# A planned attention kernel on one core: the accumulator stays open for zero-weight products until its last late tile, and the order of the work is planned anew

## The chip, the cores and the metric

The kernel runs on one core of one Trainium2 chip. The metric is the time of one execution on the device in microseconds (us); the median of the runs is what counts. A core has five engines with a queue of their own each, written here as the profile writes them: PE (TensorE, the matmuls; PEld are its weight loads), DVE (VectorE), ACT (ScalarE), POOL (GpSimd) and SP (SyncE, which here only issues DMAs).

## The reference

The input x is 2048 tokens of 512 values. Two mixers read it and a gate blends them:

```python
q, k, v = heads_of(x @ A_wqkv)                  # 32 heads of 16
p = softmax(q @ k.T * 16 ** -0.5)               # 2048 x 2048 for each head
a = merge(p @ v) @ A_wo
pq, pk = q_b @ w_phi, k_b @ w_phi               # q_b, k_b, v_b = heads_of(x @ B_wqkv)
phi = lambda y: concat(softmax(y), softmax(-y))
b = merge(phi(pq) @ (phi(pk).T @ v_b) / (phi(pq) @ phi(pk).sum())) @ B_wo
g = sigmoid((x * gate_w).sum(-1))
out = g * a + (1 - g) * b
```

Branch A is full attention: 32 x 2048 x 2048 exponentials. Branch B is linear attention with a small feature map.

## The kernel before

**Tiles.** The exponentials of branch A are cut into 2048 tiles of 128 keys by 512 queries (one head, one block of keys, one block of queries). Four heads stand side by side in TensorE's 32-row strips; a pack is four such tiles, one a head, and 16 packs with the same queries and heads (a group) share one accumulator, a bank of PSUM. There are 32 groups. For a tile the scores are one matmul of 512 columns (`_scores`, line 1044) into a PSUM bank, then comes the exponential, then the product with V (`_values`, line 1164) into the group's accumulator.

**Two ways to the exponential.** Most tiles go to ACT, in turn three and two tiles an instruction (`_exp`, line 1095), out of a ring of five PSUM banks: the next scores for a bank wait until ACT has read it. 248 tiles go to DVE instead, in batches of up to five (`_vector_batch`): DVE takes each tile's scores out of a bank (line 923), POOL cuts out a fraction (`_frac`, line 952), and DVE works out a cubic (lines 968, 969, 970) and adds it to the bits (line 938). Their products with V come in late: each is a TensorE instruction of its own, called `pvx`, that may stand in TensorE's order after the pack's own product `pv`. `SHARES` says how many tiles of each group DVE takes, `_plan_vector` spreads them over the group's packs. For group 8 it says 16, more than the 14 places there, so that two tiles of that group stand in the list twice: DVE works out 250 tiles for 248 that are used.

**The end of a group.** When the products of a group are in, its late ones too, DVE transposes the accumulator out of PSUM (line 1217), divides and transposes back (lines 1221 to 1229), and the bank is free. Three banks beside the ring serve accumulators, DVE's tiles, the projections, branch B and the output products in turn.

**The order.** No queue is written by hand. Every piece of work is an `Op` with a cost, a priority and what it depends on; `Plan.order` lists all of them engine by engine, each time taking of the operations that can start first the one with the lowest priority number, and the engines then run that order with semaphores between them. Priorities and earliest places are due times in packs, shifted by tables: `HURRY` and `EASE` (one entry for each of DVE's batches), `QEASE` (projections of queries), `LEASE` (branch B's parts), `OEASE` (output tiles), `OREL` (the last outputs), `ENDS` (the spread of DVE's tiles in the last group) and `REST` (the place of the batch of odd size).

**Zero-weight products.** Ahead of a TensorE operation `Plan.order` puts pads while the array's share of the last 2.7 us, by the plan's costs, is under 0.65 and the pad delays nothing due. A pad is four matmuls by a weight of zeros (`_fill`, line 1173), one a strip; it adds nothing to the sum. It goes into the accumulator that is open (`plan.open`), or, when none is, into a PSUM bank that is free by then; when there is neither, no pad is put. `_pv` opens the accumulator at the group's first `pv` and closes it at its last `pv`, though `pvx` of the group may still follow.

The plan's lines that decide on a pad:

```python
if have >= self.SHARE * self.SPAN or room > self.OVER * (o.kind == "col"):
    break
...
job, deps = self.open, []
if job is None:
    clear = [b for b in self.free_banks if b[1] <= first]
    if not clear:
        break
```

Of the kernel before, what the change touches and what calls it, by code (L numbers as in the profile page):

```python
# [70 lines left out]
class Plan:  # L71
# [12 lines left out]
    PORT = {"v_frac", "v_line", "v_sq", "v_cube", "v_out", "gate_z", "gate_h", "gate_b", "n_den", "n_mul", "kvbd", "b_grid", "b_rest",  # L84
            "b_max", "b_top", "b_octave", "b_square", "b_slope", "b_even", "b_odd", "b_part", "b_out", "b_sum", "b_ratio", "b_mul"}
    GUARD, GIVE, TAKE = 0.25, 0.1, 0.12
    MOVE = {}

    def __init__(self):
        self.ops = []  # L90
        self.now = -1
        self.free_banks = []
        self.loaded, self.turned = 0.0, False
        self.keep = None
        self.open = None
        self.pad = None
        self.live = False

    def op(self, eng, fn, cost, reads=(), writes=(), deps=(), name="", prio=0.0, rel=-99, kind="full",
           acquire=None, release=None, lat=None, array=None, groups=None):  # L100
        if name in self.MOVE:
            eng, cost = "POOL", self.MOVE[name](cost)
        o = Op(eng, fn, cost, name, prio, rel, kind, self.LAT[eng] if lat is None else lat, groups)
        found = {}
        for b in reads:
            for w in b.writers:
                found[id(w)] = w
        for b in writes:
            for w in b.readers or b.writers:
                found[id(w)] = w  # L110
            if b.readers:
                for w in b.writers:
                    found[id(w)] = w
        for d in deps:
            if d is not None:
                found[id(d)] = d
        found.pop(id(o), None)
        o.deps = list(found.values())
        for b in reads:
            b.readers.append(o)  # L120
        for b in writes:
            b.writers, b.readers = [o], []
        o.acquire, o.release = acquire, release
        o.array = cost if array is None else array
        self.ops.append(o)
        return o
# [265 lines left out]
class _Kernel:  # L392
# [13 lines left out]
    VREL0 = 5  # L406
    FIRST = (2, 2)
    LAST = (4,)
    OREL = 0
    ENDS = 11  # L410
    POOL = 0.00084
    SOONER = "_cube"
    TAIL = 2
    REST = 48
    HURRY = (0, 9.6, 3.1, -5.4, 16.2, -6.1, 0, -3.2, 10.5, 1.0, -8.4, 1.5, -3.1, 0.6, 12.0, 0, 9.6, 12.6, 0, -8.4, 6.7, 11.7,
              7.3, 0.7, -7.6, 2.9, 0.1, 0, 3.9, 0.3, 13.7, 4.0, 0, 3.9, -14.1, -5.6, -2.1, 7.4, 4.3, -1.8, -2.7, 18.1, -9.4,
              5.8, 4.8, 3.9, -6.0, 0, 0, 0, 0, 0, 0, 0, 0, 0, 0, 0, 0, 0)
    QEASE = (0, 4.2, -1.3, -2.9, 5.7, 0.3, 9.3, 7.6, 5.5, 9.6, -1.4, -2.2, -1.6, 9.1, 3.3, 2.1)
    LEASE = (-2.3, 3.2, 8.7, -2.0, 0, -20.0, -1.6, -2.5, -9.6, -3.3)
    OEASE = (-0.2, -4.3, 8.5, -1.3, 2.6, -5.0, 14.2, -2.3, 10.6, -2.1, 6.7, 3.8, 0.9, 0, 0, 0)  # L420
    EASE = (0, -0.9, 0, 6.0, -3.1, 3.7, 3.4, 3.9, 4.6, -1.9, -1.0, 0.1, 12, 8.0, 5.5, -12.1, -3.2, 8.6, 12, 9.8, 0, -1.0, -9.5,
              -3.3, -14, 0, 9.6, -2.8, -0.4, -10.7, 0, 10.0, -8.8, 5.2, -5.7, -4.3, -10.6, 0, -0.6, -3.0, 9.6, 3.5, -3.4, 12,
              12, -14, -4.8, 0, -0.2, 4.8, 0, -4.5, -1.6, 0, 0, 4.2, 0, 0, 0, 0)
    NBANK = 8

    def __init__(self, nc, A_x, A_wqkv, A_wo, B_wqkv, B_w_phi, B_wo, gate_w, out):
        self.nc = nc
        self.x2d = A_x.flatten_outer_dims()
        self.A_wqkv, self.A_wo = A_wqkv, A_wo
        self.B_wqkv, self.B_w_phi, self.B_wo = B_wqkv, B_w_phi, B_wo  # L430
        self.gate_w, self.out2d = gate_w, out.flatten_outer_dims()
        self.S = self.x2d.shape[0]
        self.NT = self.S // TOK
        self.NQC = self.S // QCH
        self.NPACK = self.NQC * 8 * self.NT
        self.plan = Plan()

    def build(self):
        with ExitStack() as ctx:
            self._memory(ctx)  # L440
            p = self.plan
            p.pad = lambda ot: lambda e: self._fill(e, ot)
            p.free_banks = [(b, 0.0, []) for b in range(self.NRING, self.NBANK)]
            self._loads()
            self._consts()
            self._projections()
            self._branch_b()
            self._attention()
            for o in p.order()["PE"]:
                for i in o.strips[1]:  # L450
                    o.strips[0].final[i] = o
            p.finals = self.stores
            p.emit(self.nc, ctx)
# [336 lines left out]
    def _proj_q(self, qc, cp, bank=None):  # L790
        n = qc * 4 + cp
        due = 32 * n - self.QDUE + self.QEASE[n]
        s0 = 2 * (n % (self.NQS // 2))
# [66 lines left out]
                name="gate_b", prio=24))  # L860
        self.b_hB.writers = parts

    SHARES = (0, 2, 4, 6, 2, 0, 5, 5, 16, 0, 9, 13, 4, 13, 11, 3, 11, 13, 6, 9, 9, 6, 12, 4, 11, 11, 8, 5, 12, 12, 14, 10)

    def _share(self, g):

        return self.SHARES[g]

    def _plan_vector(self):
# [9 lines left out]
        for k in range(n):  # L879
            at = (2 * k + 1) * self.ENDS // (2 * n)  # L880
            self.away.append(4 * (self.NT * last + 4 * (at // 3) + at % 3 + 1) + 3)
        left = len(self.away) - sum(self.FIRST) - sum(self.LAST)
        sizes = [self.NB] * (left // self.NB)
        sizes[self.REST:self.REST] = [left % self.NB] * (left % self.NB > 0)
        sizes = [*self.FIRST, *sizes, *self.LAST]
# [16 lines left out]
    def _vector_batch(self, number, units, due, step):  # L902
# [26 lines left out]
        n = NB * QCH  # L929
        prio = units[0] / 4 - self.VPRIO + self.HURRY[number]  # L930
        for name, cost, fn, reads, writes in self._cubic(flat(vt), flat(vf), flat(vu), n, b_vt, b_vf, b_vu):
# [170 lines left out]
    def _pv(self, p):  # L1102
        NT = self.NT
        g = p // NT
        a, kt, n = self._acc(p)
        for hook in self.hooks.get(p, ()):
            hook()
        qc, g8 = divmod(g, 8)
        block = self._block(p)
        deps, src = list(self.b_V[g8 // 2][p % NT // 4 if block is None else kt].writers), {}  # L1110
        values = list(deps)
        for u in range(4 * p, 4 * p + 4):
            if u in self.place:
                deps.append(self.exps[self.in_group[self.place[u]]])
                src[u % 4] = self.ET[:, self.place[u] % self.NSLOT, :]
        if kt == 0:
            self.ot[a] = Job()
            self.ot[a].part = block is not None
            deps += [x for u, xs in self.bits.items() if self._acc(u // 4)[0] == a - 1 for x in xs]
        else:  # L1120
            deps.append(self.pvs[p - 1])
        ot = self.ot[a]

        def run(e):
            for _ in range(o.filled):
                self._fill(e, ot)
            return self._values(e, ot, p, src, o)
        o = self.plan.op("PE", run, self._wide(4 * p), reads=[self.b_zero], deps=deps, name=f"pv{p}", prio=p + 2.5, kind="col",
                         acquire=None if kt else ot, array=0.0533 * len(src), groups=tuple(src))
        def commit(_):  # L1130
            if kt == 0:
                plan.open, plan.keep, plan.live = ot, None, True
            elif kt >= self.KEEP - NT + n and a + 1 in self.ot and all(x.start is not None for x in mine):
                plan.keep = self.ot[a + 1]
            if kt == n - 1:
                plan.open = None
        plan = self.plan
        mine = [x for u, xs in self.bits.items() if self._acc(u // 4)[0] == a for x in xs]
        o.on_commit = commit
        o.strips = (ot, tuple(src))  # L1140
        o.urgent = p >= self.NPACK - 3
        o.filler = 2 if kt and p < self.NPACK - 1 else 0
        self.pvs.append(o)
        for u in range(4 * p, 4 * p + 4):
            if u not in self.place:
                tile, made, buf = self.theirs[u]
                x = self.plan.op("PE", None, self._wide(u) - 0.13,
                                 deps=[o] + values, reads=[buf], name="pvx", prio=p + 2.6,
                                 kind="col", array=0.0533, groups=(u % 4,))
                x.fn = lambda e, u=u, tile=tile, x=x: self._values(e, ot, p, {u % 4: tile}, x)  # L1150
                x.strips = (ot, (u % 4,))
                self.late.append(x)
        if kt == n - 1:
            self._norm_a(g, [o] + self.late, ot, block and block[0] if block else None)
            self.late = []

# [417 lines left out]
    def _out_last(self, qc):  # L1574
# [3 lines left out]
        for tt in range(4):  # L1578
            t = 4 * qc + tt
            job, first = self.outs[t]  # L1580
            rel = self.NPACK - NT + 4 * tt + self.OREL
            due = self.NPACK - NT + 4 * tt + 6
# [71 lines left out]
```

## Time and profile before

| | us |
|---|---|
| median of 3 runs | 831.44 |
| the three runs | 830.63, 831.44, 832.70 |
| the profiled execution | 832.89 |
| its span, first to last instruction | 831.0 |
| ACT busy | 817.2 |
| PE busy, as modelled | 799.8 |
| DVE busy | 785.8 |
| POOL busy | 127.0 |
| mean granted clock of PE | 0.991 |

One execution was profiled, and it is slower than each of the three runs. Its span leaves out 1.89 us that lie around the instructions. The span is cut into 40 slices on the page, with a digit of busy tenths for each engine and one for the clock that PE was granted. Groups of instructions are listed by source line with their busy time, the mean of one, and the idle time of the engine just before them with what ended it. ACT is the busiest engine, and all but 2.3 us of its busy time are the 720 exponentials of line 1095. A PE that is busy in the profile need not be at its peak, since the ends of matmuls are modelled.

### The profile page before, as it was taken

The page shows a single profiled execution, that of the slowest core. Times are in us where ns is not written, and L with a number is a line of the kernel's source. Part 1 is how long each engine was busy: PE and PEld are TensorE (multiplying, and loading weights), DVE is VectorE, ACT ScalarE, POOL GpSimd, SP SyncE. Part 2 cuts the span into 40 slices and gives each one's busy share as a digit, 9 for nine tenths or more (in the row PEclk, how much of TensorE's full clock was granted, in tenths as well). Part 3 has the DMA queues.
Part 4 walks back from the last instruction along what each step waited for, and adds up shares of the span by engine and source line. Part 5 has one row for each costly group of instructions (what it writes and reads, how often), then busy time and mean ns, then how long its engine had stood idle before and what let it go on. Part 6 is the DMA issues. An engine that isn't in the chain of part 4 may idle for free.

```text
span 831.0 us, 19239 instructions
## 1 busy us (share of the span) xinstructions
PE 799.8 (96%) x8526; PEld 263.4 (32%) x8526; DVE 785.8 (95%) x1041; ACT 817.2 (98%) x725; POOL 127.0 (15%) x111
## 2 busy tenths in 40 slices
PE   9999999999989999999999999999999999999898
PEld 4323333333222222233222322223322223322244
DVE  6999999999998999999999999999999999999997
ACT  7999999999989999999999999999999999999997
POOL 3001100010112221112211212202122211122210
PEclk9999999999979999999999999999999999999999
DMA  9500000000000000031000310003110003110000
GB/s 244 165 6 8 1 8 2 1 8 1 6 2 2 8 1 3 8 65 21 1 2 10 79 23 8 8 2 65 26 21 8 2 2 64 27 27 1 2 2 28
DMA packets 49027, 19.99 MB, mean 24 GB/s; under 512 B 38704, under 2 KB 48944, under 8 KB 48944
## 3 DMA queue, kind: packets, MB, share of 16 engines
q1 hardware_dynamic: 48272, 18.58, 9.8%
q8 instruction: 66, 1.08, 0.5%
q10 hardware_dynamic: 672, 0.20, 0.1%
q14 instruction: 17, 0.14, 0.1%
HBM read 6.31 MB, written 2.10 MB: 10 GB/s over the span
## 4 chain that ended last, share of the span: by engine, by line
ACT 72%; DVE 20%; PE 6%; POOL 1%; issue 0%; DVEq 0%
ACT ET L1095 72%; DVE vu L938 3%; DVE vt L923 2%; PE ps L1044 2%; DVE vu L970 1%; DVE vf L969 1%; PE ps L1164 1%; DVE bq L1328 1%; POOL vf L952 1%; DVE VB L1312 1%; PE ps L1173 1%; DVE vt L1382 1%; DVE vu L968 1%; DVE bq L1420 1%; PE ps L720 1%; DVE V L822 1%
## 5 line engine op out<-in xcount | busy, mean ns | idle before, releaser
L1095 ACT ACTIVATE ET<-ps 128x1536 bf16<-128x1536 f32 x720 | 814.9, 1371 | 4.4 <-PE ps L1044 3.8
L1044 PE MATMUL ps<-qT,kT 32*128 32x512 bf16 (+2 forms) x2250 | 322.5, 367 | 25.0 <-ACT ET L1095 17.3
L1173 PE MATMUL ps<-kT,zero 128*32 128x512 bf16 (+1 forms) x2824 | 236.5, 386 | 0.0
L952 POOL TENSOR_SCALAR vf<-vt 128x1536 f16<-128x1536 uint8 (+1 forms) x96 | 118.9, 1254 | 651.4 <-DVE vu L938 365.4
L1164 PE MATMUL ps<-ET,V 128*32 128x512 bf16 (+2 forms) x1970 | 196.8, 368 | 1.0 <-DVE T L1217 0.5
L1044 PEld LDWEIGHTS ps<-qT,kT 32*128 32x128 bf16 x2250 | 85.8, 91 | 305.6 <-ACT ET L1095 203.0
L923 DVE TENSOR_SCALAR vt<-ps 128x512 uint32<-128x512 f32 x246 | 159.7, 680 | 14.8 <-PE ps L1044 12.3
L938 DVE SCALAR_TENSOR_TENSOR vu<-vt,vu 128x2560 int16<-128x2560 uint32 (+3 forms) x51 | 138.8, 2721 | 0.6
L1173 PEld LDWEIGHTS ps<-kT,zero 128*32 128x32 bf16 x2824 | 62.5, 95 | 98.9 <-issue 77.4
L1164 PE MATMUL ps<-vu,V 128*32 128x512 bf16 (+1 forms) x278 | 92.4, 364 | 0.1
L969 DVE TENSOR_TENSOR vf<-vf 128x2560 f16<-128x2560 f16 (+3 forms) x53 | 74.5, 1405 | 0.5
L970 DVE TENSOR_TENSOR vu<-vu,vf 128x2560 f16<-128x2560 f16 (+3 forms) x53 | 74.4, 1404 | 0.5
L1164 PEld LDWEIGHTS ps<-ET,V 128*32 128x32 bf16 x1970 | 54.7, 96 | 60.1 <-issue 32.4
L720 PE MATMUL ps<-WB,xT 128*128 128x512 bf16 x192 | 56.6, 383 | 0.6
L968 DVE TENSOR_SCALAR vu<-vf 128x2560 f16<-128x2560 f16 (+3 forms) x53 | 41.3, 780 | 3.1 <-POOL vf L952 2.9
L720 PE MATMUL ps<-xT,WA 128*128 128x512 bf16 (+1 forms) x124 | 35.1, 379 | 0.0
L1164 PEld LDWEIGHTS ps<-vu,V 128*32 128x32 bf16 x278 | 24.7, 96 | 19.3 <-issue 14.5
L1217 DVE STREAM_TRANSPOSE T<-ps 128x512 f32<-128x512 f32 (+1 forms) x35 | 23.2, 664 | 4.0 <-PE ps L1164 3.8
L1328 DVE TENSOR_SCALAR bq<-ps 128x512 bf16<-128x512 f32 x32 | 21.1, 677 | 2.0 <-PE ps L720 2.0
L720 PEld LDWEIGHTS ps<-WB,xT 128*128 128x128 bf16 x192 | 14.2, 97 | 26.9 <-issue 15.1
L816 PE MATMUL ps<-WA,xT 128*128 128x128 bf16 x256 | 18.8, 220 | 0.2
L1382 DVE TENSOR_TENSOR vt<-vt,brec 128x4096 bf16<-128x4096 bf16 (+1 forms) x10 | 18.6, 1857 | 0.0
(106 smaller groups left out, 426.6 us busy)
## 6 DMA issues: line engine op xcount, KB each, us to landing
qT<-qraw SPq DMA_DIRECT2D x120, 16.0 KB, 1.8
xn<-in_A_x_dram SPq DMA_DIRECT2D x3, 512.0 KB, 6.0
WB<-in_B_wqkv_dram SPq DMA_DIRECT2D x3, 512.0 KB, 4.9
out_dram<-WB SPq DMA_DIRECT2D x12, 128.0 KB, 1.8
WA<-in_A_wqkv_dram SPq DMA_DIRECT2D x3, 384.0 KB, 4.5
xn<-in_A_x_dram SPq DMA_DIRECT2D x2, 256.0 KB, 3.7
WoA<-in_A_wo_dram SPq DMA_DIRECT2D x1, 512.0 KB, 5.7
WoB<-in_B_wo_dram SPq DMA_DIRECT2D x1, 512.0 KB, 6.5
```

What stands on the lines that cost most here:

```text
L720: mm = op("PE", lambda e, c=c: e.matmul(self._bank(job)[:, 0:n], lhs(c), rhs(c), start=(c == 0), stop=(c == 3)), self.c_pe(n), reads=reads ...
L923: parts.append(op("DVE", lambda e, j=j, job=job: e.tensor_scalar(vt[:, j, :], self._bank(job), SCALE * LOG2E * 2.0 ** 24, 2.0 ** 31, op0=A ...
L938: self.last_out = o = op("DVE", lambda e: e.scalar_tensor_tensor(out=flat(vu).bitcast(I16), in0=flat(vt), scalar=2.0 ** -17, in1=flat(vu), ...
L952: "POOL", lambda e, a=at, n=n: e.tensor_scalar(vf[:, a:a + n, :], vt[:, a:a + n, :].bitcast(U8).rearrange("p n (q h) -> p n q h", h=4)[:, ...
L968: lambda e: e.tensor_scalar(vu, vf, CUBE, SQUARE, op0=ALU.mult, op1=ALU.add), [b_vf], [b_vu]),
L969: ("_sq", two, lambda e: e.tensor_tensor(vf, vf, vf, ALU.mult), [b_vf], [b_vf]),
L970: ("_cube", two, lambda e: e.tensor_tensor(vu, vu, vf, ALU.mult), [b_vf, b_vu], [b_vu]),
L1044: ins = e.matmul(out[u][:, cols], self.kT[32 * i:32 * i + 32, cp, kt * TOK:(kt + 1) * TOK], self.qT[32 * i:32 * i + 32, s, q], start=True, ...
L1095: o = plan.op("ACT", lambda e: e.activation(self.ET[:, a % NS:a % NS + n, :], self.ps[:, a % NR:a % NR + n, :], ACT.Exp, scale=SCALE), sel ...
L1164: ins = e.matmul(self._bank(ot)[32 * i:32 * i + 32, to], self.V[:, kt, g8 // 2, v0:v0 + 32], tile[:, cols], start=first and j == 0, stop=o ...
L1173: ins = e.matmul(self._bank(ot)[32 * i:32 * i + 32, lo:QCH], self.zero[:], self.kT[:, 0, lo:QCH], start=False, stop=False, tile_position=( ...
L1328: [lambda e, b, k=k: e.tensor_scalar(bq[:, k].rearrange("p (g s v) -> p g s v", g=8, s=2)[:, :, 0, :], b.rearrange("p (g v) -> p g v", g=8 ...
```

## The change

Three things change: `_pv` closes a group's accumulator only when the last of its late products has been placed; `Plan` can shift the priority of single operations by name and number (`NUDGE`, 65 entries); and all the tables of the order hold other numbers. Two knobs without use (`MOVE`, `NBANK`) go. `SHARES` now sums to 244 instead of 246, with no group over 14.

```diff
-        if name in self.MOVE:
-            eng, cost = "POOL", self.MOVE[name](cost)
+        n = self.made[name] = self.made.get(name, 0) + 1
+        prio += self.nudge.get((name, n), 0.0)
...
-    OREL = 0
-    ENDS = 11
+    OREL = 3
+    ENDS = 10
...
-    REST = 48
-    HURRY = (0, 9.6, 3.1, -5.4, 16.2, -6.1, 0, -3.2, 10.5, 1.0, -8.4, 1.5, -3.1, 0.6, 12.0, 0, 9.6, 12.6, 0, -8.4, 6.7, 11.7,
...
+    REST = 53
+    HURRY = (0.5, -7.6, 5.1, -6.5, 6.3, -11.8, 0, -8.0, 0, -17.8, -0.4, -1.2, -12.9, 25, 0, 8.1, 12.3, 0, 0.4, 10.0, 3.8, -1.8,
...
+    NUDGE = {
+        'b_max': {11: 3.7, 23: 22.2, 67: 10.7, 74: -19.5, 79: 13.2},
...
+        'pq': {34: 13.8, 40: 29.9, 43: -1.4, 53: -11.9, 69: -25.9, 73: 8.8, 77: 14.1, 85: -7.9, 88: -0.9, 101: 13.5,
+            120: 13.9},
...
+        'vqk': {75: 4.6, 78: -22.3, 124: 17.0, 130: -21.7, 149: 19.2, 156: 14.5},
+    }
...
-    SHARES = (0, 2, 4, 6, 2, 0, 5, 5, 16, 0, 9, 13, 4, 13, 11, 3, 11, 13, 6, 9, 9, 6, 12, 4, 11, 11, 8, 5, 12, 12, 14, 10)
+    SHARES = (0, 2, 4, 6, 0, 5, 2, 8, 10, 5, 11, 10, 8, 8, 9, 12, 9, 10, 2, 9, 6, 11, 9, 14, 7, 10, 5, 13, 11, 7, 12, 9)
...
-            if kt == n - 1:
+            if kt == n - 1 and not late:
                 plan.open = None
-        plan = self.plan
+        plan, late = self.plan, []
...
         if kt == n - 1:
+            late = list(self.late)
+
+            def close(_):
+                if plan.open is ot and all(x.start is not None for x in late):
+                    plan.open = None
+            for x in late:
+                x.on_commit = close
```

The computation, the tiles and the formulas are the same.

More of the change, by code (lines that the diff above doesn't have):

```diff
@@ L86 @@
     GUARD, GIVE, TAKE = 0.25, 0.1, 0.12
-    MOVE = {}
     def __init__(self):
@@ L91, in __init__ @@
         self.now = -1
+        self.made, self.nudge = {}, {}
         self.free_banks = []
@@ L413 @@
     TAIL = 2
-    REST = 48
-    HURRY = (0, 9.6, 3.1, -5.4, 16.2, -6.1, 0, -3.2, 10.5, 1.0, -8.4, 1.5, -3.1, 0.6, 12.0, 0, 9.6, 12.6, 0, -8.4, 6.7, 11.7,
[L416 to L424, printed above, removed]
+    REST = 53
+    HURRY = (0.5, -7.6, 5.1, -6.5, 6.3, -11.8, 0, -8.0, 0, -17.8, -0.4, -1.2, -12.9, 25, 0, 8.1, 12.3, 0, 0.4, 10.0, 3.8, -1.8,
+              -7.4, 0.7, 7.3, 25, 8.8, 25, 5.8, -6.9, 7.6, 3.4, -25, -14.5, 1.2, -7.3, -7.5, -20.6, -17.2, 21.6, -12.2, -4.6,
+              0, 10.0, -0.9, -12.6, 11.2, -4.7, -4.7, 0.8, 0, 0, 0, 0, 0, 0, 0, 0, 0, 0)
@@ new lines @@
+    QEASE = (0, -10, -4.8, 6.8, 6.6, 10.5, 16, 11.0, -7.8, 7.8, -3.9, -6.4, -9.2, 10.5, 8.8, 16)
+    LEASE = (-1.6, 3.6, 4.0, 0.7, -0.7, -14.9, 6.4, 16.5, -4.9, 3.4)
+    OEASE = (11.6, 1.0, -4.4, 23.0, 18.8, 11.8, 17.2, 6.8, 5.3, -3.9, 1.0, 3.6, 8.7, 0, 0, 0)
+    EASE = (-1.8, -6.9, 0, 0, 0, -0.2, 4.4, -4.4, 0.6, -6.3, 3.6, 0, 0, -14.4, -8.5, 1.4, -5.7, -1.4, -10.4, 0, -6.6, 5.8, 0,
+              -4.2, -8.4, 7.4, -4.4, -6.5, 0, -5.6, 8.6, 2.8, -8.3, 10.0, 0, -4.3, 0, -5.7, -8.9, 0, 0, -1.5, -1.1, 5.6, 8.1,
+              -3.6, 0, 7.0, -0.1, 0, 0, -4.5, -1.6, 0, 0, 4.2, 0, 0, 0, 0)
@@ new lines @@
+    NUDGE = {
+        'b_max': {11: 3.7, 23: 22.2, 67: 10.7, 74: -19.5, 79: 13.2},
+        'b_out': {3: 19.0, 11: 12.0, 17: 21.2},
+        'b_part': {17: 21.2},
+        'b_ratio': {2: -30.6},
+        'b_rec': {8: 13.7},
+        'b_slope': {6: -11.3},
+        'b_square': {6: -16.5, 8: 11.6},
+        'b_sum': {25: 27.1},
+        'b_top': {7: -9.2, 9: 10.4},
+        'bn_mul': {8: 43.5},
+        'bv': {33: 6.1, 39: 10.5, 45: 19.5, 57: 8.1},
+        'den': {13: 12.4},
+        'kproj': {44: 0.8, 45: 6.5},
+        'kproj_ev': {6: 7.4, 13: -15.7},
+        'kv': {5: 11.6},
+        'n_den': {9: -17.4},
+        'n_mul': {10: 6.8, 14: 20.1},
+        'n_rec': {3: 3.0},
+        'n_t1': {20: 17.9, 26: 6.9},
+        'num': {14: 12.6},
+        'pq': {34: 13.8, 40: 29.9, 43: -1.4, 53: -11.9, 69: -25.9, 73: 8.8, 77: 14.1, 85: -7.9, 88: -0.9, 101: 13.5,
+            120: 13.9},
+        'pq_ev': {14: -22.9},
+        'qproj_ev': {7: -7.8, 9: -10.7},
+        'v_bits': {42: 17.3},
+        'v_cube': {6: -3.1, 17: -11.8},
+        'v_line': {10: 6.4, 46: -18.6},
+        'vproj': {33: 3.1, 52: -14.5, 61: -3.2},
+        'vproj_ev': {10: -13.3, 12: -7.6},
+        'vqk': {75: 4.6, 78: -22.3, 124: 17.0, 130: -21.7, 149: 19.2, 156: 14.5},
+    }
@@ L436, in __init__ @@
         self.plan = Plan()
+        self.plan.nudge = {(name, n): by for name, moved in self.NUDGE.items() for n, by in moved.items()}
     def build(self):
@@ L442, in build @@
             p.pad = lambda ot: lambda e: self._fill(e, ot)
-            p.free_banks = [(b, 0.0, []) for b in range(self.NRING, self.NBANK)]
+            p.free_banks = [(b, 0.0, []) for b in range(self.NRING, 8)]
             self._loads()
```

## The prediction, as put on record before the result

> **What bounds the kernel now.** I read the 40 slices first, then the groups by line, then ACT's waits, and last the busy time of each engine in stretches of 3.41 us.
>
> ```profile
> PE 799.8 (96%) x8526; PEld 263.4 (32%) x8526; DVE 785.8 (95%) x1041; ACT 817.2 (98%) x725; POOL 127.0 (15%) x111
> ...
> DVE  6999999999998999999999999999999999999997
> ACT  7999999999989999999999999999999999999997
> ...
> PEclk9999999999979999999999999999999999999999
> ...
> L1095 ACT ACTIVATE ET<-ps 128x1536 bf16<-128x1536 f32 x720 | 814.9, 1371 | 4.4 <-PE ps L1044 3.8
> ```
>
> ACT is the bound: 814.9 us of exponentials in a span of 831.0, idle for 4.4 us in front of them, nearly all because scores (L1044) were late. One exponential takes 814.9 / 720 = 1.132 us. The slice where ACT drops to 8 is the one in which PE's clock drops to 7. ACT's own order of time, asked for around there and near the end, puts figures to it (start, duration, what, idle before):
>
> ```profile
> 238.15 1.02 ACT L1095 ACTIVATE ET<-ps 128x1024 bf16<-128x1024 f32 x1 [0.54 <-PE ps L1164]
> 239.53 1.45 ACT L1095 ACTIVATE ET<-ps 128x1536 bf16<-128x1536 f32 x1 [0.36 <-PE ps L1044]
> 242.32 1.02 ACT L1095 ACTIVATE ET<-ps 128x1024 bf16<-128x1024 f32 x1 [1.33 <-PE ps L1044]
> 243.62 1.45 ACT L1095 ACTIVATE ET<-ps 128x1536 bf16<-128x1536 f32 x1 [0.28 <-PE ps L1044]
> ```
>
> ```profile
> 784.73 1.45 ACT L1095 ACTIVATE ET<-ps 128x1536 bf16<-128x1536 f32 x1 [0.54 <-PE ps L1044]
> 786.64 15.93 ACT L1095 ACTIVATE ET<-ps 128x1024 bf16<-128x1024 f32 x14 [0.47 <-PE ps L1044]
> ```
>
> That is 0.54 + 0.36 + 1.33 + 0.28 = 2.51 us at the first place and 0.54 + 0.47 = 1.01 us at the second. The rest of the 4.4 is 0.62 + 0.21 us at the start (in front of the exponentials at 7.29 and 8.96). Anywhere else ACT never waits. The stretches around both places (length, then busy us and instructions of PE, PEld, DVE, ACT, POOL, then the granted clock):
>
> ```profile
> 226.14:229.55 3.41, 2.71 (x32) 0.74 (x28) 3.41 (x3) 3.41 (x5) 0.00 (x0) 1.00 0.10 25
> 229.55:232.96 3.41, 1.72 (x9) 0.45 (x9) 3.41 (x5) 3.41 (x4) 0.00 (x0) 1.00 0.00 0
> 232.96:236.38 3.42, 3.28 (x16) 0.88 (x15) 3.22 (x6) 3.42 (x5) 1.65 (x2) 0.50 0.00 0
> ...
> 632.56:635.97 3.41, 2.60 (x35) 0.86 (x39) 3.41 (x4) 3.41 (x4) 1.13 (x1) 1.00 0.11 27
> ...
> 779.10:782.51 3.41, 2.49 (x24) 0.62 (x21) 3.38 (x3) 3.41 (x4) 0.44 (x1) 1.00 0.01 2
> 782.51:785.92 3.41, 3.25 (x34) 1.36 (x34) 2.41 (x5) 2.87 (x3) 2.04 (x2) 0.50 0.02 5
> ```
>
> After a stretch with 1.72 us of PE busy the clock is at a half, until 243.20; after one with 2.49 us it is at a half for 3.41 us; after 2.60 us it stays whole. So the bound has two parts: the exponentials, and two half-clock stretches in which scores came late.
>
> **The change part by part.**
>
> *Exponentials.* Both orders hold 720 ACT exponentials for 1800 tiles (2048 less 248), in the same turn of three and two. ACT's 814.9 us stay.
>
> *Two tiles worked out twice go.* The order has two L923 fewer, and the odd batch shrinks from three tiles to one. By the rows of before, L923 costs 0.61 us apiece from start to start, and the cubic of three against one 0.87 + 0.44 + 0.86 + 0.81 + 1.64 = 4.62 against half of a batch of two's 0.60 + 0.40 + 0.65 + 0.66 + 1.14 = 3.45, about 1.8; DVE's queue sums to 781.7 instead of 785.8 us. DVE ends no chain by its total (45 us idle), so I book nothing at the end. What it hides behind is ACT; were DVE the bound, it would be worth 4.1 us.
>
> *Zero-weight products.* Their 512-wide matmuls go from 2792 to 2804, three more sets of four. Eight took 0.61 us, twelve 0.83 us, so a set costs 0.21 us: 0.6 us on an engine whose weight loads wait 203.0 us for ACT. No cost while a set stands where PE waits; if all three stood right ahead of scores that are late, 0.6 us.
>
> *The accumulator open for late tiles.* Between a group's last `pv` and its last `pvx` the order of before has 48 sets, that of after 76. At neither half-clock place would this rule have helped: there the group had no late product left, the next accumulator was not yet open, and the banks were taken. At 228.62 to 232.72 the order of before has the scores of four exponentials with nothing between them, and around 782 two. Those places must be cured by the new order.
>
> *The new order.* In the order of TensorE I counted the turns of the array between the scores of one exponential and the next: 512 columns are a turn, instructions on different strips side by side share one. At 0.21 us a turn, three exponentials (3.40 us, about one stretch of the table) hold at the least, from exponential 10 to 700:
>
> - before: 3 turns at exponentials 196 to 200 (the place at 229 us), 6 turns at 195, 201, 551 and 681 (633 us, whole clock, and 780 us, half clock), 7 turns at 645 and 680, otherwise 8 and more;
> - after: 6 turns once, at exponential 348, about 7.3 + 348 x 1.132 = 401 us; otherwise 8 and more.
>
> So the deep hole goes (around exponential 198 there now stand the products of the next group, four matmuls for branch B's values and three for queries), the second goes, and one place is left of a depth that cost nothing once and a half-clock stretch once. Gain: 2.51 + 1.01 = 3.52 us. From below the term is 0 (the half clock comes all the same), and the new place can give back up to 1.01 us. I take 3.52, as the row at 632.56 with its whole clock is the nearest to the places that remain.
>
> *Is PE overfull elsewhere?* Over four exponentials (4.53 us) both orders hold at most 4.33 us of turns, over six (6.79 us) 6.05 and 6.09. I book nothing.
>
> *Does DVE come late?* For each of 53 batches I took the exponentials between its last scores and its first product, at 1.132 us, less the DVE work queued from its last L923 to its L938, by the durations of before. The thinnest leads are 0.3, 0.4, 0.8, 0.8, 0.8 us before and 0.4, 0.4, 0.6, 0.7, 0.7 after, the medians 2.6 and 2.5. ACT did not wait for such a product outside the half-clock stretches before; I book nothing.
>
> *SP, POOL, start, end.* All engines begin alike (TensorE's first 75 operations among them). SP's queue has the same 68 entries with outputs and queries' DMAs exchanged from the 31st on; ACT never waited for one. After the last scores there is one late product fewer and one zero set more; the chain from the last exponential (ends 826.09) through L1217 to L1229, the last output products, the copy and the store to 831.0 is the same. OREL moves output products between the last scores: up to six turns (1.3 us) now stand ahead of the last ones, which have the next ACT instruction and the one under way, 1.58 + 1.16 us. Nothing, or at most 0.4 us.
>
> **Sum.** Span 831.0 - 3.52 = 827.5 us. Around it lie 832.89 - 831.0 = 1.89 us: **829.4 us**. The profiled execution is 1.45 us above the median and above every run shown, so the runs probably lost less at these two places; against the median the gain is only 831.44 - 829.4 = 2.0 us (0.25%).
>
> The half clock held for 10.24 us and 3.41 us, and 539.31 us lie between the end of the first and the start of the second: 3, 1 and 158 times 3.413 us. So it is decided on a fixed grid, and how a hole falls on the grid can differ from run to run: that fits runs of 830.63 to 832.70. The Trainium skill (TensorE: Matmul & The Clock Gate, Part 1) says so too: a free-running window of 3413 ns, with half rate or whole. The trace agrees.
>
> **Rivals.**
>
> 1. *One short half-clock stretch remains*, at exponential 348 or another place of eight turns that waits make deeper. For: of two six-turn places one had it. Price as at 782: 1.01 us, so 830.4 us.
> 2. *The count of turns is not what gates the clock.* Then the new order changes nothing: the half clock comes back somewhere and costs what it does now, 831.4 (the median) to 832.9 us (the profiled execution). Against: both stretches follow the two emptiest of the grid's windows. The same page (Why this matters for your kernels) speaks for this rival: it asks only that no idle gap passes about 3 us, and by that rule PE with 24 matmuls in 779.10 to 782.51 should have kept its clock. The trace disagrees: the clock halved.
> 3. *Late products block TensorE: slower.* TensorE takes its order strictly; a `pvx` whose L938 is late holds the scores behind it, and ACT runs dry. Place: the batches with a lead of 0.4 to 0.7 us (around exponentials 312 to 333 and 636 to 656). Price: one L938 (2.82 us) for each batch that is late by an instruction. One such batch eats most of the gain (829.4 + 2.8 = 832.2); from two on the kernel is slower: 829.4 + 5.6 = 835.0 us. Against: the leads are no thinner than before's.
>
> **How the numbers follow.** I call 0.3% (2.5 us: below 828.95 or above 833.9) what a measurement can tell. The forecast, both holes gone and nothing new, has a chance of 0.58. It lies 0.4 us above that bound, and whether an unprofiled run carries all of the 1.89 us is not shown; I put 0.40 below the bound and 0.18 above. Rival 1 has 0.20, rival 2 0.12, rival 3 0.10. Faster 0.40, same 0.18 + 0.20 + 0.12 = 0.50, slower 0.10. The range: down to 828.2 (1.2 us under the forecast, should the profile itself cost what parts it from the runs), up through rival 1 to 832.0, which takes in the lower part of rival 2; rival 3 and the rest of rival 2 are left out.
>
> **What would show it.** Right: PEclk without a digit under 9 before the last slice, idle in front of L1095 about 0.9 us instead of 4.4, all of it at the start, and a span of 827.5. Rival 1: one stretch of 3.41 us at 0.50, ACT idle there. Rival 2: ten or more us at 0.50 where the count shows no hole. Rival 3: PE waiting for L938 and ACT idle with a whole clock. Wrong would also be a tail longer than 4.9 us after the last exponential.

## The result, and the profile after

| | before | after |
|---|---|---|
| median of 6 runs, us | 832.23 (830.63 to 833.82) | 828.85 (828.41 to 830.29) |
| ratio to before | | 0.9961, 95% interval 0.9946 to 0.9976 |
| span of the profiled execution, us | 831.0 | 826.5 |
| mean granted clock of PE | 0.991 | 1.000 |

The kernel became faster by 0.39% (0.24% to 0.54%); the forecast was 829.4 us in the range 828.2 to 832.0. Six runs of before have a median 0.8 us above that of the three known at the time. The prediction set its bound for faster at 828.95 us and gave 0.40 to a time below it and 0.50 to one near the old time; 828.85 us is below that bound by 0.1 us, so on which side of it the time fell is luck. From 832.23 us the same 0.3% lies at 829.7 us.

The page of after, with the lines that answer those of before (busy us and share, the 40 slices, the exponentials with their idle time at the end):

```profile
PE 789.5 (96%) x8494; PEld 261.8 (32%) x8536; DVE 781.7 (95%) x1039; ACT 816.3 (99%) x725; POOL 127.4 (15%) x111
...
DVE  6999999999999999999999999999999989999986
ACT  7999999999999999999999999999999999999997
...
PEclk9999999999999999999999999999999999999999
...
L1127 ACT ACTIVATE ET<-ps 128x1536 bf16<-128x1536 f32 x720 | 814.0, 1389 | 0.6 <-PE ps L1076 0.5
```

Line 1127 is the line 1095 of before. No slice of ACT or of the clock is under 9 inside any more, and of 4.4 us of idle time in front of the exponentials 0.6 is left, 0.5 of it at the start. The stretches of 3.41 us on the clock's grid, at the two old places (229 and 780 us), at the place that the prediction feared (401 us) and at the emptiest of all (500 us); columns as before, the clock third from the end:

```profile
227.16:230.57 3.41, 2.99 (x37) 1.05 (x35) 3.41 (x4) 3.41 (x4) 1.14 (x1) 1.00 0.00 0
...
401.24:404.65 3.41, 3.06 (x33) 0.80 (x33) 3.41 (x3) 3.41 (x4) 0.00 (x0) 1.00 0.00 0
500.22:503.63 3.41, 2.82 (x43) 1.14 (x39) 3.41 (x6) 3.41 (x4) 0.00 (x0) 1.00 0.00 0
...
779.86:783.27 3.41, 3.33 (x43) 1.06 (x41) 3.41 (x3) 3.41 (x5) 0.62 (x1) 1.00 0.02 5
```

PE is never below 2.82 us there, and the clock is whole. To see where the time went I set the start of each of the 720 exponentials in one trace against the other: before is 0.3 us behind or less up to exponential 200 (0.1 there), 3.0 us at 240, between 3.0 and 3.6 us from there to 680, and 4.6 us at the last. So all of the 4.5 us between the spans comes from the two half-clock places, about 3.1 us from the first and 1.3 us from the second; start and tail (4.89 and 4.91 us after the last exponential) are equal.

### The profile page after: what moved, and what is told of

The parts are those of the page before. It is cut to its first block, busy times and chain, and to the rows that moved or that the text cites. A ratio compares the mean times of both kernels' runs of the same rounds, so it can differ in the third digit from the quotient of the medians.

```text
span 826.5 us, 19222 instructions
## 1 busy us (share of the span) xinstructions
PE 789.5 (96%) x8494; PEld 261.8 (32%) x8536; DVE 781.7 (95%) x1039; ACT 816.3 (99%) x725; POOL 127.4 (15%) x111
## 3 DMA queue, kind: packets, MB, share of 16 engines
q1 hardware_dynamic: 48272, 18.58, 10.2%
## 4 chain that ended last, share of the span: by engine, by line
ACT 98%; PE 1%; DVE 0%; issue 0%
ACT ET L1127 98%; PE ps L704 0%; PE ps L786 0%; PE ps L723 0%; PE ps L1076 0%; PE ps L802 0%; DVE qT L813 0%; PE ps L1203 0%; DVE xT L735 0%; DVE xT L1641 0%; PE ps L1631 0%; DVE T L1256 0%; DVE onTA L1268 0%; DVE T L1264 0%; DVE rinv L1262 0%
## 5 line engine op out<-in xcount | busy, mean ns | idle before, releaser
L1076 PE MATMUL ps<-qT,kT 32*128 32x512 bf16 (+2 forms) x2248 | 318.8, 364 | 26.9 <-ACT ET L1127 16.7
L1212 PE MATMUL ps<-kT,zero 128*32 128x512 bf16 x2836 | 235.8, 384 | 0.1
L1076 PEld LDWEIGHTS ps<-qT,kT 32*128 32x128 bf16 x2248 | 84.0, 91 | 303.3 <-ACT ET L1127 216.0
L1203 PE MATMUL ps<-vu,V 128*32 128x512 bf16 (+1 forms) x275 | 90.1, 362 | 0.0
L752 PE MATMUL ps<-WB,xT 128*128 128x512 bf16 x164 | 47.9, 382 | 3.0 <-issue 1.3
```

Source lines behind the costliest of these rows:

```text
L752: mm = op("PE", lambda e, c=c: e.matmul(self._bank(job)[:, 0:n], lhs(c), rhs(c), start=(c == 0), stop=(c == 3)), self.c_pe(n), reads=reads ...
L1076: ins = e.matmul(out[u][:, cols], self.kT[32 * i:32 * i + 32, cp, kt * TOK:(kt + 1) * TOK], self.qT[32 * i:32 * i + 32, s, q], start=True, ...
L1203: ins = e.matmul(self._bank(ot)[32 * i:32 * i + 32, to], self.V[:, kt, g8 // 2, v0:v0 + 32], tile[:, cols], start=first and j == 0, stop=o ...
L1212: ins = e.matmul(self._bank(ot)[32 * i:32 * i + 32, lo:QCH], self.zero[:], self.kT[:, 0, lo:QCH], start=False, stop=False, tile_position=( ...
```

## The experiments

The theory: an empty stretch on PE halves its clock, the scores behind it come late, and ACT loses that time. Rivals: the gain is the order as such (what stands where, with the clock a bystander); or it is the rule of the open accumulator; or it is DVE's lighter load. Ratios are to before on the same chip in the same set: 831.29 us for the kernels with filled holes, the rule alone and the tables alone; 831.97 us for the tile worked out twice and the changed kernel beside it; 831.59 us for the other four. Differences in us to the changed kernel's 828.85 go across sets, in which before's medians differ by up to 0.9 us, and are no better than that.

### Fill the holes and change nothing else

After the planner had ordered the kernel before, zero-weight sets were put into TensorE's order behind named scores; the transposition that reads the accumulator waits for them.

```diff
+            p.order()
+            self._cover({7: ((196, 3), (197, 3), (198, 3), (199, 2), (200, 2), (201, 2), (202, 2))})
...
+            for k, n in after:
+                at = next(i for i, o in enumerate(queue) if o.name == f"qk{k}") + 1
+                for _ in range(n):
+                    x = Op("PE", self._fill_into(g), 0.2133, "pad", 0.0, -99, "col", 0.2, Plan.ALL)
+                    queue.insert(at, x)
+                    read.deps.append(x)
```

> The kernel before in its own order, with 17 more zero-weight sets put right behind the scores of exponentials 196 to 202, into group 7's finished accumulator that DVE has not read yet (its transpose waits for them). Nothing else moves. Theory (an empty stretch on TensorE halves its clock, and the scores then come late): the half clock at 233 us goes, the exponentials of before stand 3.1 us later behind that place than the changed kernel's, so 832.2 - 3.1 = 829.1 us; the short half-clock stretch near 780 us stays. Rival (the gain comes from the order of the other work, the clock is a bystander): 832.2 us. Rival (turns are not what gates the clock): the half clock still comes at 233 us.

The second kernel has `29: ((679, 2), (681, 1), (682, 2))` as well.

> As before_fill1, with 5 more sets near 780 us, behind the scores of exponentials 679, 681 and 682, into group 29's accumulator. Theory: no half clock at all until the last microseconds, exponentials within 0.5 us of the changed kernel's all along, so 828.9 us, as fast as the change with none of its tables and without its rule. Rival (order): 832.2 us.

Measured: 829.76 us (ratio 0.9974, 0.9962 to 0.9987) with the first hole filled, 829.56 us (0.9970, 0.9958 to 0.9982) with both. The clock is whole in both profiles. In the one with the first hole filled, the windows where before had one with 1.72 us of PE are full, and the second hole is still there:

```profile
228.14:231.55 3.41, 3.38 (x51) 0.97 (x44) 3.41 (x2) 3.41 (x4) 0.00 (x0) 1.00 0.04 10
231.55:234.96 3.41, 3.21 (x42) 0.88 (x39) 2.81 (x6) 3.41 (x4) 0.00 (x0) 1.00 0.02 5
...
777.68:781.10 3.42, 2.39 (x29) 0.71 (x31) 3.42 (x3) 3.42 (x4) 0.90 (x1) 1.00 0.00 0
```

The twelve runs with one hole filled fall into seven from 829.05 to 829.83 us, all with a mean granted clock of 1.000, and five from 830.74 to 830.93 us, all with 0.998; with both filled all twelve lie between 829.29 and 829.87 us at 1.000, where before spreads over 830.2 to 835.0 us at 0.990 to 0.996. So the theory holds, and the second hole halves the clock in some executions only. The last row above shows that PE's busy time alone does not decide it: 2.39 us kept the clock whole here, 2.49 us halved it in before.

But the exponentials of both kernels are still 1.0 us behind the changed kernel's at exponential 203 and stay about so (1.0 and 1.3 us at the last). ACT, PE and DVE there, with both holes filled (L1112 is the exponential, L1061 scores, L1181 the product with V, L1190 a zero-weight product, L940 the first DVE step of a tile):

```profile
238.15 3.28 ACT L1112 ACTIVATE ET<-ps 128x1024 bf16<-128x1024 f32 x3 [0.57 <-PE ps L1181]
```

```profile
232.15 0.62 PE L1190 MATMUL ps<-kT,zero 128*32 128x512 bf16 x8
232.70 0.70 PE L1061 MATMUL ps<-qT,kT 32*128 32x512 bf16 x5
233.12 2.48 DVE L940 TENSOR_SCALAR vt<-ps 128x512 uint32<-128x512 f32 x4 [0.60 <-PE ps L1061]
...
237.10 0.38 PE L1061 MATMUL ps<-qT,kT 32*128 32x512 bf16 x1 [0.18 <-DVE vt L940]
237.70 0.61 PE L1181 MATMUL ps<-ET,V 128*32 128x512 bf16 x7 [0.21 <-DVE vt L940]
```

ACT waits for a product, not for scores: since the last product at 228.11 us none has run, and ET, which holds exponentials until their product with V, has 25 tiles, which are ten exponentials or 11.3 us. The product waited for a bank that the ninth of ten L940 freed at 237.64 us. So of the 3.1 us at the first place the filling took away 2.1. The other 1.0 us stays open: before has the same wait (0.54 us at 238.15), but there DVE waits three times 0.1 us for scores at half clock and the product takes 0.61 us instead of 0.39. Here the added sets delay it, since two of them stand ahead of the scores at 232.70, and DVE waits 0.60 us for these and 0.15 us for later ones. Without these 0.75 us the ninth L940 would have ended at about 236.9 us, too early to stop ACT (an estimate from these rows). The 1.0 us can thus be the price of the filling and is not shown to be the order.

### The tile worked out twice

To see whether DVE's double work is in that 1.0 us, the two tiles that stand twice were read only in part the first time, whose outcome nobody uses; both holes were filled.

```diff
+            o.fn = lambda e, vt=vt, job=job: e.tensor_scalar(
+                vt[:, 0:8], self._bank(job)[:, 0:8], SCALE * LOG2E * 2.0 ** 24, 2.0 ** 31, op0=ALU.mult, op1=ALU.add)
```

> As before_fill2 (which measured 829.56 us, its exponentials 1.0 us behind the changed kernel's from 202 and 203 on, with the clock whole), but the two tiles that stand twice in the list of before are read only for 8 of their 512 columns the first time, which nobody uses; the result is the same. One of the two is the second of ten L940 in a row there, behind which the first product of group 8 waits for a bank, while 25 tiles of ET are full. Theory (the rest of the gap is that run of ten, and the tile worked out twice is a part of it): the wait there shrinks by 0.6 us, 829.0 us. Rival (DVE's saving hides behind ACT, as the prediction had it): 829.6 us.

Measured: 829.47 us (829.27 to 829.51), against 829.56; the wait at exponential 203 is the same 0.57 us. My theory that the tile worked out twice holds the run of ten up fell: DVE (L960 is its line 940 here, L481 the shortened read) is done sooner and then waits itself, for scores (L1081) behind zero-weight products (L1210).

```profile
232.30 0.61 PE L1210 MATMUL ps<-kT,zero 128*32 128x512 bf16 x8
232.85 0.70 PE L1081 MATMUL ps<-qT,kT 32*128 32x512 bf16 x5
```

```profile
231.27 0.63 DVE L960 TENSOR_SCALAR vt<-ps 128x512 uint32<-128x512 f32 x1
231.81 0.15 DVE L481 TENSOR_SCALAR vt<-ps 128x8 uint32<-128x8 f32 x1
233.27 2.48 DVE L960 TENSOR_SCALAR vt<-ps 128x512 uint32<-128x512 f32 x4 [1.30 <-PE ps L1081]
```

The next tile's scores stand in TensorE's order behind ACT's own scores and behind two of the sets that this experiment put in, and come no earlier. Putting those sets behind DVE's scores was not tried, nor moving the product, whose bank comes from those tiles. So this run says nothing of DVE's double work in an order without filling. The changed kernel beside it:

> The changed kernel beside fill2_once on the same chip: 828.9 us, its exponentials with no wait but the first; if the theory holds, fill2_once stands within 0.5 us of it.

Measured: 828.98 us (ratio 0.9960, 0.9943 to 0.9976). That is 0.49 us below the 829.47, just inside the 0.5 us; the theory's step, a shorter wait at 203, did not come all the same. Of its seven runs two have a granted clock under 1.000: 828.98 us (0.998) and 830.12 us (0.997). So the changed kernel too loses a little of its clock in some executions.

### Make a hole in the changed kernel

```diff
+            self._thin(lambda k: 504 <= k < 516)
...
+            if o.name == "pad" and drop(k):
+                continue
```

> The changed kernel in its own order, without the 21 zero-weight sets that stand between the scores of exponentials 504 and 516; they add nothing to any sum. Three exponentials then hold 5 to 7 turns there, 13 exponentials long. Theory: the window's busy time falls to about half, the clock halves for 3.41 us or more near 580 us, and the scores behind come late: 1 to 3 us, so 830 to 832 us. Rival (the clock is a bystander, filler is worth nothing): 828.9 us with the clock whole or not.

Measured: 830.73 us (0.9991, 0.9982 to 1.0), 1.9 us above the changed kernel's 828.85; by the ratios to before (0.9991 against 0.9961) 2.5 us. Its grid there:

```profile
577.80:581.21 3.41, 1.63 (x18) 0.49 (x16) 2.90 (x6) 3.41 (x4) 0.73 (x1) 1.00 0.05 10
581.21:584.62 3.41, 2.76 (x19) 0.53 (x16) 3.41 (x5) 3.41 (x4) 0.00 (x0) 0.50 1.15 211
584.62:588.04 3.42, 3.37 (x20) 0.65 (x17) 3.31 (x3) 3.42 (x4) 0.66 (x1) 0.50 0.47 87
588.04:591.45 3.41, 3.41 (x31) 0.96 (x28) 2.66 (x6) 3.11 (x3) 1.82 (x2) 0.50 0.02 5
591.45:594.86 3.41, 3.41 (x38) 1.43 (x34) 3.15 (x5) 2.25 (x2) 0.00 (x0) 0.50 0.00 0
```

Cause and cost lie 10 us apart. The hole (1.63 us of PE busy) halves the clock at 581.21; ACT (the fourth busy figure) loses nothing for 6.8 us, because the order asks little of PE there, and then 2.2 us (most of it at exponentials 516 to 518) when the work gets dense and the clock is still at a half. This is the theory by itself: nothing but zeros was taken away.

### The rule alone, and the tables alone

The rule alone is the diff's last hunk put into the kernel before:

> The kernel before with only the accumulator's later closing; all tables as before, so the planner orders anew from TensorE's operation 1651 on. The count of turns: the hole at exponentials 196 to 200 stays (3 turns), the one at 681 goes (nothing under 8 turns there). Theory: the long half clock at 233 us stays, the short one near 780 us goes: 832.2 - 1.4 = 830.8 us. Rival (the rule is the gain): 828.9 us.

Measured: 834.43 us (1.0029, 1.0016 to 1.0042). The half clock at 232 us stays and the one near 780 goes; the exponentials end 1.4 us nearer to the changed kernel's than before's do, as expected. But the tail grew from 4.9 to 7.6 us, which I had not looked at. The last of DVE's batches comes after the last exponential (L938 of DVE, the late product L1171 of PE, the transposition L1224):

```profile
823.54 2.28 DVE L938 SCALAR_TENSOR_TENSOR vu<-vt,vu 128x2048 int16<-128x2048 uint32 x1
826.70 0.32 DVE L1224 STREAM_TRANSPOSE T<-ps 128x128 f32<-128x128 f32 x1 [0.88 <-PE ps L1171]
```

```profile
825.87 0.23 PE L1171 MATMUL ps<-vu,V 128*32 128x128 bf16 x1 [0.19 <-DVE vu L938]
```

ACT's last exponential ended at 825.22; L938 ends at 825.82. The rule re-ordered everything behind its first effect, and with the old tables the last batch of DVE came out behind the last exponential.

The tables alone close the accumulator at the last `pv` again:

> The changed kernel with the accumulator closed at the last pv again; its tables as changed, so the planner orders anew from TensorE's operation 646 on. The count of turns: new holes of 2 to 4 turns at exponentials 283 and 284, 639 to 641 and 657 to 661, and behind the last of them 7.2 us of turns in 4.5 us. Theory: three stretches of half clock, at 3.1 us each (the price of the deep hole of before) 838 us, and more for the overfull place: 838 to 845 us. Rival (the tables are the gain, the rule does nothing): 828.9 us.

Measured: 855.88 us (1.0283, 1.0259 to 1.0307). Three half-clock stretches came where the count had its holes (6.8, 10.2 and 13.7 us long), but they are not the main cost. What ACT waited for:

```profile
ACT ET L1127 <- PE ps L1196: 13.2, 3, 8.1
ACT xT L1637 <- PE ps L1624: 8.9, 1, 8.9
ACT ET L1127 <- PE ps L1076: 5.9, 10, 1.1
```

13.2 us are waits for products (L1196), that is for a free tile of ET, and 5.9 us for scores; the tail is 11.7 us. The exponentials end 20.5 us later than the changed kernel's and the tail is 6.8 us longer: 27.3 us. I had priced only the holes. In these two orders neither the rule nor the tables gain anything without the other.

### The rule's own zero-weight sets taken out

The changed order as it is, without the sets for which the accumulator is kept open:

```diff
+        drop = {i for j, i0 in last.items() for i in range(i0, end.get(j, 0)) if queue[i].name == "pad"}
+        self.plan.queues["PE"] = [o for i, o in enumerate(queue) if i not in drop]
```

> The changed kernel in its own order, without the 76 zero-weight sets that stand between a group's last pv and its last late product, which is the time for which the change keeps the accumulator open. Holes of 5 turns for three exponentials at 220 to 222 and 663 to 664, of 6 at 218, 219, 635, 643, 644, 660 to 662. Theory: two to four stretches of half clock near 255, 725 and 755 us, at 1.4 to 2.1 us each, so 832 to 836 us: the rule's sets are what keeps the clock whole in this order. Rival (the tables alone are the gain): 828.9 us.

Measured: 833.90 us (831.21 to 837.36; 1.0024, 1.0008 to 1.0039), 5 us above the changed kernel. Three half-clock stretches, at 258.8, 361.2 and 760.6 us, put the exponentials back by 1.6, 1.7 and 2.5 us. Two of them are at expected holes; the one at 361 us is at none of them, and none came near 725 us, so the count of turns both misses places and names some that cost nothing.

### DVE's load in one place

```diff
+            x = Op("DVE", o.fn, o.cost, "v_bits", 0.0, -99, "full", 0.138)
+            x.deps = list(o.deps)
+            o.deps.append(x)
+            queue.insert(queue.index(o), x)
```

> The changed kernel with seven of DVE's L955 (the first step of a tile) done twice, between exponentials 343 and 353: about 4.3 us more for DVE, the amount that the change saves it, in one place; the result is the same. Theory by the prediction's sum (DVE's total hides behind ACT): no more than 0.5 us, 829.3 us. Rival (the late products have leads of about 2.5 us at the median, and DVE can't give 4.3 us at once): a late product holds TensorE's order, 4.3 - 2.5 = 1.8 us, 830.7 us.

Measured: 833.89 us (1.0028, 1.0018 to 1.0039), 5.0 us above the changed kernel: both figures were too low. PE and ACT at the place (L1013 is the last step of the cubic, L1087 the scores), PE at a second one, and then the grid:

```profile
403.82 1.03 PE L1087 MATMUL ps<-qT,kT 32*128 32x512 bf16 x5 [2.33 <-DVE vu L1013]
...
404.94 2.49 ACT L1138 ACTIVATE ET<-ps 128x1536 bf16<-128x1536 f32 x2 [1.63 <-PE ps L1087]
```

```profile
417.79 0.60 PE L1087 MATMUL ps<-qT,kT 32*128 32x512 bf16 x2 [0.69 <-DVE vu L1013]
```

```profile
399.91:403.32 3.41, 1.52 (x21) 0.29 (x9) 3.34 (x4) 3.40 (x4) 0.00 (x0) 1.00 0.02 5
403.32:406.74 3.42, 2.92 (x23) 0.55 (x27) 3.42 (x3) 1.79 (x2) 0.00 (x0) 0.50 0.00 0
```

DVE late makes PE wait for 2.33 us, that empties a window of the grid (1.52 us busy), the clock halves for 6.8 us, and the scores that are already late run slowly. What PE waited for is not what the rival says: no product of a DVE tile is late there. The scores of DVE's next tiles are, which the plan lets in only when the cubic of an earlier batch is done (`SOONER`), and they hold the order in front of ACT's scores. Set against the changed kernel, ACT is 1.9 us late at the first exponential behind the wait (404.94 us), 1.9 us more are lost by the time the clock is whole again, and 1.1 us at the second wait of the same kind. The 45 us that DVE is idle over the span gave no cover at all.

### No zero-weight products

> The changed kernel in its own order without any zero-weight set (709 of them go; no sum changes). Theory: holes of 4 to 6 turns all along, the clock at a half for a good part of the span, the array then with less than it needs, over 20 us slower. Rival (the clock is a bystander): 828.9 us or less, as 150 us of TensorE's turns go.

Measured, in two runs: 891.92 us (1.0725, 1.0697 to 1.0754), with 0.743 of the clock on average. The page's engine line: ACT, busy 99% of the changed kernel's span, is at 94%, and PE has 2836 matmuls less to do.

```profile
PE 811.6 (91%) x5700; PEld 223.6 (25%) x5700; DVE 787.8 (89%) x1039; ACT 832.4 (94%) x725; POOL 126.9 (14%) x111
```

709 sets of zeros, 709 x 0.21 = 150 us of the array's turns, buy 891.9 - 828.85 = 63 us.

## Why the prediction was right, point by point

**What bounds the kernel: right.** Behind its start, the two half-clock places were all that parted ACT's exponentials from an unbroken row. One part of the reading is too simple: the 0.54 us at 238.15 are a wait for a product with ET full, not for late scores.

**The gain of 3.52 us: right in kind, a fifth too small.** The traces give 4.5 us. The term took the idle time in front of six late exponentials. Their starts are late by 0.76 + 0.48 + 1.46 + 0.40 + 0.67 + 0.59 = 4.36 us, counted from the usual distance of starts (medians 1.330 us behind an exponential of three tiles, 0.904 behind one of two). An exponential that runs alone takes 1.45 or 1.02 us, so in an unbroken row each overlaps the next by 0.12 us, and a late one loses that overlap before any idle time shows. Of six, five lost 0.12 to 0.13 us more than the idle column says and one 0.22. The Trainium skill (ScalarE: Activation LUTs, What ACT_TABLE_LOAD costs) puts the overlap of ACT instructions in a row at about 93 ns; here it is 0.12 us.

**"Those places must be cured by the new order": not shown to be needed.** 22 zero-weight sets in the old order bring the clock back at both; what they leave of the 3.1 us at the first place, 1.0 us, is a full ET with the clock whole, and how much of that the old order would cost without the sets stays open.

**The count of turns: right for this change**; at the place of six turns (401 us) nothing happened. It is rough, as the sets taken out show, and so is busy time (2.39 us whole, 2.49 us half). Over the ten traces that show clock changes, the array's share of a grid window, worked out from the columns and starts of its matmuls, was 0.27 to 0.54 in the windows inside the span after which a whole clock halved; none of 0.55 or more was followed by that, and between 0.46 and 0.54 both occur. The changed kernel's emptiest window, at 500 us, has 0.53, within that range.

**Rival 1: did not come in the six runs of the result, all at 1.000;** in the later set it fits the two runs of seven with a clock of 0.998 and 0.997.

**Rival 2: fell.** With it fell the rule of the Trainium skill behind it (TensorE: Matmul & The Clock Gate, Why this matters for your kernels). No window inside the span that halved the clock was idle, and filling alone cured it. The Trainium skill (TensorE: Matmul & The Clock Gate, Terms) prices half clock at its time by one half. In the kernel with the hole an estimate by that is 13.65 x 0.5 = 6.8 us; the trace shows 2.2, and ACT loses none of it in the first half of the 13.65 us.

**DVE's saving booked at nothing: nothing contradicts it.** DVE's busy time fell to 781.7 us as summed, and the spans differ by what the two half-clock places cost; 829.47 against 829.56 us says little, as DVE then waited for scores behind the filling. **Its cover was named wrongly**: neither ACT's length nor DVE's 45 idle us cover work that is put in one place. 4.3 us more there cost 5.0 us. The leads that the prediction worked out, from a batch's last scores to its first product, did not decide it either: the scores of the next tiles wait for DVE sooner. Rival 3 did not come in the changed kernel, where no exponential waits but the first ones; its price of 2.8 us for one late batch is near the 2.33 us that PE waited here, but leaves out the half clock that follows.

**The accumulator's rule "would not have helped": right for the first place, wrong in effect for the second**: with the rule alone no set stands there by the rule, but the planner's new order filled the place. In the changed order its sets are worth 5.0 us.

**Time outside the span: right.** The profiled execution took 828.5 us for a span of 826.5, 2.0 us more against the assumed 1.89. That the runs of before lose less at the two places than the profiled one (0.991) is right for most: in the set of 29 beside the filled kernels 18 have a clock of 0.993 to 0.996 and take 830.16 to 832.09 us, 11 have 0.990 to 0.992 and take 832.39 to 835.03.

## What to carry to other kernels

Look for a dip of PE's clock before looking for idle engines: ask for busy times on the grid of 3.41 us, find the emptiest window ahead of the dip, and expect the cost some microseconds behind it, where work is dense again. Zeros multiplied into an accumulator that nobody has read yet are a filler that needs no bank; here 22 sets took 1.7 us off and nearly all the scatter. They are better put behind scores that another engine waits for than ahead of them, which was not tried here. In an order that a planner makes, one small rule moves everything behind it: judge the rule and its tables together, the tail too, and look for the cover of a late engine in what waits for each piece of its work, buffers included, never in its idle total.

## What the runs showed of the hardware

The half clock ended only after a window in which the array, at half clock, was at work for 0.79 of the time or more: windows of up to 0.89 also kept it at a half, and none under 0.79 ended it inside the span. In the kernel with the hole the four windows of half clock have 0.63, 0.78, 0.73 and 0.88, and only the last ended it: so a hole of one window (1.63 us busy) brought four. The runs of before scatter with the share of the clock that they lose, 830.2 us at 0.996 to 835.0 us at 0.990, and with both holes filled lie within 0.6 us. That this share depends on how a hole falls on the grid fits the runs but is not shown. Nor is all scatter the clock's: the changed kernel's runs at 1.000 spread over 828.21 to 830.29 us. Part of such a spread can come from the start, as the first exponential begins between 6.97 and 7.95 us in the twelve traces.
